# Attention with two mixtures of experts on one core: one wide GpSimd product for the strided heads of batch 0

## The chip, the core and the metric

The kernel runs on one core of a Trainium2 chip. A core has five engines that work through queues of their own, in order: TensorE (PE in the profile; its weight loads are PEld), VectorE (DVE), ScalarE (ACT), GpSimd (POOL) and SyncE (SP), which here issues most of the transfers. The metric is the device time of one execution in microseconds; lower is better. The time given is the median of three runs.

## The reference, cut to what matters

Three stages follow each other. Only the first, the attention, is touched.

```python
def _attn_ref(q, k, v):                       # 4 batches, 8 heads, 576 positions, 64 wide
    scores = scale * np.matmul(q, k.transpose(0, 1, 3, 2))
    rel = pos[:, None] - pos[None, :]
    mask_local = (rel >= 0) & (rel < 32)
    mask_strided = (rel >= 0) & (pos[None, :] % 32 == pos[:, None] % 32)
    # heads 0-3 take mask_local, heads 4-7 mask_strided
    scores = np.where(masks[None], scores, -1e9)
    attn = softmax(scores)                    # with 1e-9 added to the sum
    return np.matmul(attn, v)

x = attn_out.transpose(0, 2, 1, 3).reshape(2304, 512)
x = _moe_ref(x, w_in, w_out, g_ln)            # x @ w_in, softmax gate, layer norm, @ w_out
return _moe2_ref(x, ...)                      # top-1 of 8 experts, relu MLP, scaled by the gate
```

A strided head attends only to positions with the same remainder by 32. In the kernel a strided head's 576 positions are read as 8 groups of 72; within a group, 4 residues of 18 positions each see each other.

## The kernel before

**Tiling.** The attention goes through heads in pairs, and each pair through four units (two sets of tiles, two heads). Batch 0 takes its strided pairs first (PAIRS[0] is 2, 3, 0, 1), so the first eight units of the program are strided units of batch 0, with four tiles of 72 x 72 each; the next eight are its local units with 96-row tiles. Then come batches 1 to 3, mixed with the first mixture of experts, and from some 375 us on the experts of the second.

**A strided unit of batch 0** is made by `compact` (line 327). TensorE computes for each tile only the four residue blocks of 18 x 18 (L335), one block in each group of 32 partitions. VectorE adds the mask (L342), takes the maximum (L344), subtracts it (L345); ScalarE takes the exponential (L347); VectorE sums (L349) and takes the reciprocal (L350). Then GpSimd spreads the blocks: four products (L353), one per residue, each over 32 partitions, write the 18 probabilities of a row into every fourth column of a buffer `spread` of 72 columns, which four memsets cleared once at the start (L693). The columns of the other residues stay zero.

**Its transposition** (`probs_T`, L424) is a matmul with the spread tile as weights and, as the moving operand, 72 of the 128 columns of the identity, read with a stride of 32 elements so that rows come out in the order of positions. ScalarE copies the result to SBUF (L432), and TensorE multiplies with v (L441). The result goes to xTH and xTL (L453, L454).

**What shares the queues.** While this runs, the two weight matrices w_in and w_out, which are stored as 64-bit floats, are loaded in pieces of 512 KB by SyncE (L217) into three buffers and split by ScalarE and VectorE (L223, L231, L232, L234, L242, L243); for three of the first w_out pieces the scaling L225 is GpSimd's. GpSimd also fills `zrow` (L183) and `tabi` (L186, L187), which take their turn in the same three buffers and which SyncE stores to memory (L198, L199) ahead of the w_out loads. The local units use GpSimd for their normalisation (L413).

**Order.** The program is written as a sequence of slots, but the order in which an engine's queue holds the instructions is set when the program is built, by a planner that simulates the instructions' times. What one instruction takes in that simulation can move others.

Of the kernel before, what the change touches and what calls it, by code (L numbers as in the profile page):

```python
# [9 lines left out]
F32 = mybir.dt.float32  # L10
# [4 lines left out]
ALU = mybir.AluOpType  # L15
AX = mybir.AxisListType
# [12 lines left out]
def tile_attention_moe_moe2(  # L29
# [15 lines left out]
    nc = tc.nc  # L45
# [3 lines left out]
    P = 128  # L49
# [5 lines left out]
    SP_ = S // SG  # L55
    EPS = 3
    PITCH = P + EPS + 1
    QUAD = 32
    RES = STRIDE // SG
    NR = SP_ // RES  # L60
# [47 lines left out]
    ident = cst.tile([P, P], F32, name="ident")  # L108
# [23 lines left out]
    def flip_tile(out_, in_, eye):  # L132
        return nc.tensor.transpose(out_, in_, eye)  # L133
# [8 lines left out]
    def build_masks():  # L142
        nc.gpsimd.memset(rebias, 2.0 ** -112)
        nc.gpsimd.memset(zeros, 0.0)
        for t in range(2):
            m = maskL[:QT, t]
            nc.gpsimd.memset(m, 0.0)
            nc.gpsimd.affine_select(
                out=m, in_=m, pattern=[[-1, P]], compare_op=ALU.is_ge,
                fill=NEG, base=STRIDE, channel_multiplier=1)  # L150
            nc.gpsimd.affine_select(
                out=m, in_=m, pattern=[[1, P]], compare_op=ALU.is_gt,
                fill=NEG, base=0, channel_multiplier=-1)
            if t == 0:
                nc.gpsimd.memset(m[:, 0:STRIDE], NEG)
        rank = mp.tile([P, 1], I32, name="rank", tag="e")
        rankf = mp.tile([P, 1], F32, name="rankf", tag="e")
        nc.gpsimd.iota(rank, pattern=[[0, 1]], base=0, channel_multiplier=1)
        nc.gpsimd.iota(maskC, pattern=[[1, NR]], base=0, channel_multiplier=0,
                       allow_small_or_imprecise_dtypes=True)  # L160
        nc.vector.tensor_scalar(rank, rank, QUAD - 1, None, ALU.bitwise_and)
        nc.vector.tensor_copy(rankf, rank)
        nc.vector.tensor_scalar(maskC, maskC, rankf, NEG, ALU.is_gt, ALU.mult)
        apart = mp.tile([SP_, SP_], I32, name="apart", tag="so")
        nc.gpsimd.iota(apart, pattern=[[-1, SP_]], base=P, channel_multiplier=1)
        nc.vector.tensor_scalar(apart, apart, STRIDE // SG - 1, None, ALU.bitwise_and)
        nc.vector.tensor_scalar(maskS, apart, 0, NEG, ALU.is_gt, ALU.mult)
        nc.gpsimd.affine_select(
            out=maskS, in_=maskS, pattern=[[-1, SP_]], compare_op=ALU.is_ge,
            fill=NEG, base=0, channel_multiplier=1)  # L170
# [157 lines left out]
    def compact(tiles, j, qT, kT):  # L328
        nt = len(tiles)
        sp_ = ps.tile([P, 4, P], F32, name="S", tag="h")  # L330
        for i, t in enumerate(tiles):
            q0 = (j * SG + t) // 2 * SP_
            for r in range(RES):
                q1, k1 = q0 + r, STRIDE + q0 + r
                nc.tensor.matmul(  # L335
                    sp_[r * QUAD:(r + 1) * QUAD, i, :NR], qT[:, q1:q1 + RES * (QUAD - 1) + 1:RES],
                    kT[:, t % 2, k1:k1 + RES * (NR - 1) + 1:RES], start=True, stop=True)
        exw, px = exs[turn[0] % len(exs)], spread[turn[0] % len(spread)]
        turn[0] += 1
        ex = exw[:, :nt, EPS + 1:EPS + 1 + NR]  # L340
        mx = st.tile([P, 4], F32, name="mx")
        nc.vector.tensor_tensor(  # L342
            ex, sp_[:, :nt, :NR], maskC.unsqueeze(1).to_broadcast([P, nt, NR]), ALU.add)
        nc.vector.reduce_max(mx[:, :nt], ex, axis=AX.X)  # L344
        nc.vector.tensor_tensor(  # L345
            ex, ex, mx[:, :nt].unsqueeze(2).to_broadcast([P, nt, NR]), ALU.subtract)
        nc.scalar.activation(ex, ex, AF.Exp, scale=SCALE)  # L347
        rd = st.tile([P, 4], F32, name="rd")
        nc.vector.reduce_sum(rd[:, :nt], exw[:, :nt, EPS:EPS + 1 + NR], axis=AX.X)  # L349
        nc.vector.reciprocal(rd[:, :nt], rd[:, :nt])  # L350
        for r in range(RES):
            rows = slice(r * QUAD, (r + 1) * QUAD)
            nc.gpsimd.tensor_tensor(  # L353
                px[rows, :nt, r:SP_:RES], ex[rows],
                rd[rows, :nt].unsqueeze(2).to_broadcast([QUAD, nt, NR]), ALU.mult)
        return px, P, SP_, None

    def scores(b, hp, tiles, j, qT, kT):
# [58 lines left out]
    def probs_T(tiles, ex, nq, nk, den):  # L417
        nt = len(tiles)
        pt = ps.tile([P, 4, P], F32, name="pP", tag="T")
        if den is None:  # L420
            cols = ident.rearrange("p (r a) -> p a r", a=QUAD)[:, 0:NR, :]
            nq = nk
            for i in range(nt):
                nc.tensor.matmul(  # L424
                    pt[:nk, i, :nq].rearrange("p (a r) -> p a r", r=RES), ex[:, i, :nk], cols,
                    start=True, stop=True)
        else:
            for i in range(nt):
                flip_tile(pt[:nk, i, :nq], ex[:nq, i, :nk], ident[:nq, :nq])
        pT = at.tile([P, 4 * SP_], F32, name="pT", bufs=3)  # L430
        pT = pT[:, 0:nt * nq].rearrange("p (t q) -> p t q", q=nq)
        nc.scalar.copy(pT[:nk, :nt, :nq], pt[:nk, :nt, :nq])  # L432
        return pT
# [22 lines left out]
    def attention_slots():  # L456
# [25 lines left out]
        def stage_a(n):  # L482
            if n < len(units):
                b, hp, tiles, j = units[n]
                if b == 0 and hp >= H // 4:
                    live[n] = compact(tiles, j, *tr[n // 4])
                else:
                    live[n] = scores(b, hp, tiles, j, *tr[n // 4])
                    normalise(b, hp, len(tiles), *live[n])
# [8 lines left out]
        def stage_p(n):  # L498
            z = n - LAG
            if 0 <= z < len(units):  # L500
                b, hp, tiles, j = units[z]
                ex, nq, nk, den = live.pop(z)
                pts[z] = (probs_T(tiles, ex, nq, nk, den), nk if den is None else nq, nk)
# [179 lines left out]
    at = atstack.enter_context(tc.tile_pool(name="at", bufs=2))  # L683
# [4 lines left out]
    spread = []  # L688
    for i in range(2):
        pair = mp.tile([P, 2, 4, SP_], F32, name=f"spread{i}", tag="nL")  # L690
        spread.extend([pair[:, 0], pair[:, 1]])
    for x in spread:
        nc.gpsimd.memset(x, 0.0)  # L693
    kzs = [at.tile([P, 2, STRIDE + S], F32, name=f"kz{i}", bufs=1) for i in range(2)]
    for kz in kzs:
        nc.vector.memset(kz[:, :, 0:STRIDE], 0.0)
# [11 lines left out]
    def take(upto):  # L708
        nonlocal taken
        while taken < upto:  # L710
            next(slots, None)
            taken += 1

    build_masks()
    wout = list(range(KF))
    for i, at_ in enumerate(W_IN_AT):
# [629 lines left out]
```

## Time and profile before

| | us |
|---|---|
| median of three runs | 653.43 |
| the three runs | 651.59, 653.43, 659.1 |
| profiled execution, its own time | 650.67 |
| its span, first to last instruction | 649.0 |
| TensorE busy in the span | 606.4 (93%) |
| VectorE busy | 363.7 (56%) |
| ScalarE busy | 315.1 (49%) |
| GpSimd busy | 180.4 (28%) |

All rows quoted here come from that one profiled execution. Times in them count from the start of the span. A name such as L353 is a line of the kernel before. In a row, `out<-in` names what an instruction writes and reads, and a bracket at the end tells how long its engine idled before it and what ended the wait. A busy share is an average over stages that differ much, so the stretches are read one by one.

### The profile page before, as it was taken

The numbers are of one execution on the slowest core, as the hardware profiler recorded it, in microseconds if no ns is written. First come the engines' busy times: TensorE is split into PE (matmuls) and PEld (weight loads), VectorE is DVE, ScalarE is ACT, GpSimd is POOL, SyncE is SP. The second block draws the span as 40 slices with busy tenths as digits, with TensorE's granted clock in tenths as the row PEclk, the third lists the DMA queues.
The fourth block names the chain that finished last, engine by engine and source line by source line (L and its number), as shares of the span: only waits on it lengthen the run. The fifth ranks groups of instructions, "written<-read, shape, count | busy, mean of one in ns | idle before, by whom it ended". The sixth has DMA issues, their size and how long they took to land. (4 is left out here: it accounts for less than half of the span.)

```text
span 649.0 us, 13048 instructions
## 1 busy us (share of the span) xinstructions
PE 606.4 (93%) x4760; PEld 545.8 (84%) x4760; DVE 363.7 (56%) x1155; ACT 315.1 (49%) x685; POOL 180.4 (28%) x256
## 2 busy tenths in 40 slices
PE   5777999999999999999999999999999999999992
PEld 3666888999998988988888999989888888899892
DVE  5987698577767767667479753216354553121120
ACT  4679676567655667567356431224335352221220
POOL 4765364012432342112004312410121213012101
PEclk9997889999999999999999999999999999999997
DMA  8875221033211212110035300344546553012010
GB/s 219 207 216 146 77 84 38 19 88 100 74 54 37 70 43 77 54 36 3 27 106 178 99 34 19 103 163 129 183 135 207 144 202 101 20 49 66 19 47 24
DMA packets 54770, 59.97 MB, mean 92 GB/s; under 512 B 39312, under 2 KB 39312, under 8 KB 54674
## 3 DMA queue, kind: packets, MB, share of 16 engines
q1 hardware_dynamic: 47810, 42.52, 23.0%
q0 software_dynamic: 4272, 11.57, 5.7%
q10 hardware_dynamic: 2592, 4.72, 2.0%
q8 instruction: 46, 0.75, 0.5%
q14 instruction: 50, 0.41, 0.2%
HBM read 49.05 MB, written 10.26 MB: 91 GB/s over the span
## 5 line engine op out<-in xcount | busy, mean ns | idle before, releaser
L930 PE MATMUL py<-w2H,winL 128*128 128x512 f32 x288 | 92.1, 395 | 0.0
L970 PE MATMUL pf<-xTH,w1H 128*128 128x256 f32 x288 | 82.2, 286 | 1.4 <-ACT yo L1068 1.4
L970 PE MATMUL pf<-xTL,w1H 128*128 128x256 f32 x288 | 81.7, 284 | 0.7 <-DVE xTL L909 0.7
L970 PE MATMUL pf<-xTH,w1L 128*128 128x256 f32 x288 | 81.4, 283 | 0.0
L977 DVE SCALAR_TENSOR_TENSOR winL<-pf,winL 128x512 fp32r<-128x512 f32 x36 | 24.9, 691 | 94.4 <-ACT winL L976 94.3
L976 ACT ACTIVATE winL<-pf 128x512 fp32r<-128x512 f32 x36 | 21.5, 598 | 85.9 <-PE pf L970 85.2
L930 PEld LDWEIGHTS py<-w2H,winL 128*128 128x128 f32 x288 | 53.4, 188 | 10.6
L413 POOL TENSOR_TENSOR ex<-ex,rd 96x384 f32<-96x384 f32 (+1 forms) x48 | 40.5, 844 | 73.9 <-DVE rd L407 45.7
L536 PE MATMUL ph<-winH,xTH 128*128 128x512 f32 x144 | 58.6, 407 | 1.3 <-ACT xTH L453 0.8
L970 PEld LDWEIGHTS pf<-xTH,w1H 128*128 128x128 f32 x288 | 56.1, 195 | 3.1 <-issue 1.9
L536 PE MATMUL ph<-winL,xTH 128*128 128x512 f32 x144 | 57.6, 400 | 0.0
L970 PEld LDWEIGHTS pf<-xTL,w1H 128*128 128x128 f32 x288 | 56.2, 195 | 1.3 <-DVE xTL L909 1.1
L536 PE MATMUL ph<-winH,xTL 128*128 128x512 f32 x144 | 56.5, 399 | 0.0
L970 PEld LDWEIGHTS pf<-xTH,w1L 128*128 128x128 f32 x288 | 56.2, 195 | 0.0
L372 PE MATMUL S<-kz,qT 128*96 128x128 f32 (+1 forms) x384 | 48.2, 266 | 6.2 <-ACT kz L326 4.7
L936 POOL DMA_INDIRECT out_dram<-yo,idx x14 | 14.1, 1005 | 143.0 <-ACT yo L935 125.6
L372 PEld LDWEIGHTS S<-kz,qT 128*96 128x96 f32 (+1 forms) x384 | 41.6, 165 | 8.6 <-ACT kz L326 5.3
L391 POOL TENSOR_TENSOR ex<-ex,mx 96x384 f32<-96x384 f32 (+1 forms) x32 | 25.3, 791 | 81.7 <-DVE mx L387 40.2
L595 PE MATMUL pa<-woH,nH 128*128 128x264 f32 x144 | 42.1, 292 | 1.2 <-ACT nH L584 1.2
L595 PE MATMUL pa<-woH,nL 128*128 128x264 f32 x144 | 42.5, 295 | 0.0
L595 PE MATMUL pb<-woH,nL 128*128 128x256 f32 x144 | 41.1, 285 | 0.0
L595 PE MATMUL pb<-woL,nH 128*128 128x256 f32 x144 | 41.0, 284 | 0.0
(262 smaller groups left out, 1610.0 us busy)
## 6 DMA issues: line engine op xcount, KB each, us to landing
raw<-in_moe_w_dram SPq DMA_DIRECT2D x36, 512.0 KB, 3.6
y_d<-yt ACTq DMA_DIRECT2D x18, 256.0 KB, 2.2
raw<-in_moe_w_in_dram SPq DMA_DIRECT2D x8, 512.0 KB, 6.8
raw<-in_moe_w_out_dram SPq DMA_DIRECT2D x8, 512.0 KB
vn<-in_v_dram SPq DMA_DIRECT2D x16, 160.0 KB, 3.3
qn<-in_q_dram SPq DMA_DIRECT2D x8, 288.0 KB
kn<-in_k_dram SPq DMA_DIRECT2D x8, 288.0 KB
vn<-in_v_dram SPq DMA_DIRECT2D x8, 288.0 KB
```

The lines of the kernel that those rows point to most:

```text
L372: nc.tensor.matmul(sp_[:nq, i, :nk], qT[:, q0:q0 + nq], kT[:, half, k0:k0 + nk], start=True, stop=True)
L391: eng.tensor_tensor(ex[:nq, :nt, :nk], ex[:nq, :nt, :nk], mx[:nq, :nt].unsqueeze(2).to_broadcast([nq, nt, nk]), ALU.subtract)
L413: nc.gpsimd.tensor_tensor(ex[:nq, :nt, :nk], ex[:nq, :nt, :nk], rd[:nq, :nt].unsqueeze(2).to_broadcast([nq, nt, nk]), ALU.mult)
L536: nc.tensor.matmul(ph, a[:, c, ts_], w[:, c, cs], start=n == 0, stop=n == 3 * KD - 1)
L595: nc.tensor.matmul(p, a[:, f], w[:, f, cols], start=n == 0, stop=n == 3 * KF - 1)
L930: nc.tensor.matmul(p, a[:, f, s], x, start=n == 0, stop=n == 3 * KF - 1)
L936: nc.gpsimd.indirect_dma_start(out=out[:, :], out_offset=indirect(idx[:, col, 2:3].bitcast(U32)), in_=o, in_offset=None, bounds_check=NT - ...
L970: mm = nc.tensor.matmul(p[:, u], a[:, c, fs], x[:, c], start=n == 0, stop=n == 3 * KD - 1)
L976: last[0] = (nc.scalar.activation(hH[:, f2s], p, AF.Relu), nc.vector.scalar_tensor_tensor(hL[:, f2s], p, 0.0, hH[:, f2s].bitcast(F32), ALU ...
L977: nc.vector.scalar_tensor_tensor(hL[:, f2s], p, 0.0, hH[:, f2s].bitcast(F32), ALU.max, ALU.subtract))
```

## The change

GpSimd's four products per strided unit of batch 0 become one product over all 128 partitions. It computes all four columns of each group of four, and its second factor `rdm` holds the reciprocal for the row's own residue and zero for the other three; `rdm` is made by a new VectorE product of the reciprocal with a constant `own` (128 x 4, one where the partition belongs to the residue). As every column is written, the four memsets of `spread` go. The 72 columns of the identity that L424 reads with a stride are copied once into a dense constant `sel`, which the transposing matmuls then read.

```diff
@@ build_masks
+        nc.gpsimd.tensor_copy(
+            sel.rearrange("p (a r) -> p a r", r=RES),
+            ident.rearrange("p (r a) -> p a r", a=QUAD)[:, 0:NR, :])
+        nc.vector.reduce_sum(own, ident.rearrange("p (r a) -> p r a", a=QUAD), axis=AX.X)
@@ compact
-        for r in range(RES):
-            rows = slice(r * QUAD, (r + 1) * QUAD)
-            nc.gpsimd.tensor_tensor(
-                px[rows, :nt, r:SP_:RES], ex[rows],
-                rd[rows, :nt].unsqueeze(2).to_broadcast([QUAD, nt, NR]), ALU.mult)
+        rdm = at.tile([P, 4, RES], F32, name="rdm")
+        nc.vector.tensor_tensor(
+            rdm[:, :nt], rd[:, :nt].unsqueeze(2).to_broadcast([P, nt, RES]),
+            own.unsqueeze(1).to_broadcast([P, nt, RES]), ALU.mult)
+        nc.gpsimd.tensor_tensor(
+            px[:, :nt].rearrange("p t (a r) -> p t a r", r=RES),
+            ex.unsqueeze(3).to_broadcast([P, nt, NR, RES]),
+            rdm[:, :nt].unsqueeze(2).to_broadcast([P, nt, NR, RES]), ALU.mult)
@@ probs_T
-            cols = ident.rearrange("p (r a) -> p a r", a=QUAD)[:, 0:NR, :]
             nq = nk
             for i in range(nt):
-                nc.tensor.matmul(
-                    pt[:nk, i, :nq].rearrange("p (a r) -> p a r", r=RES), ex[:, i, :nk], cols,
-                    start=True, stop=True)
+                nc.tensor.matmul(pt[:nk, i, :nq], ex[:, i, :nk], sel, start=True, stop=True)
@@ where the buffers are made
-    for x in spread:
-        nc.gpsimd.memset(x, 0.0)
+    own = at.tile([P, RES], F32, name="own", bufs=1)
+    sel = at.tile([P, SP_], F32, name="sel72", bufs=1)
```

The pool `at` gives a tile two buffers unless it says otherwise, so `rdm` has two.

## Rows read from the trace of the kernel before

**Rows 1.** Stage windows: length, each engine's busy time (instructions), clock, DMA share, GB/s
```profile
20.00:40.00 20.00, 16.30 (x219) 14.34 (x219) 19.89 (x58) 15.35 (x34) 17.32 (x32) 1.00 0.72 205
...
80.00:375.00 295.00, 287.97 (x2389) 260.21 (x2389) 214.43 (x779) 182.26 (x428) 87.56 (x111) 0.99 0.23 65
375.00:649.00 274.00, 258.50 (x1709) 234.45 (x1708) 89.94 (x165) 77.68 (x133) 48.89 (x49) 0.98 0.31 97
```

**Rows 2.** Tile spread: ns min/median/max, first and last start; who waited for it
```profile
L353 POOL TENSOR_TENSOR spread<-ex,rd x32: 313/626/823, 14.1 to 39.6; 32x72 f32<-32x72 f32 x32
L693 POOL MEMSET spread<- x4: 328/338/342, 1.0 to 2.2; 128x288 f32 x4
...
  PEld pP L424: 3.1, 2
```

**Rows 3.** GpSimd's time line: start, length, operation, idle before and its end
```profile
23.41 12.46 POOL L353 TENSOR_TENSOR spread<-ex,rd 32x72 f32<-32x72 f32 x20
...
36.87 0.61 POOL L187 MEMSET tabi<- 128x176 int32 x1
...
43.91 1.04 POOL L225 TENSOR_TENSOR mag<-raw,rebias 128x512 f32<-128x512 f32 x1 [3.98 <-DMA raw<-in_moe_w_out_dram]
```

**Rows 4.** TensorE's time line
```profile
30.05 1.23 PE L424 MATMUL pP<-ident,spread 128*72 128x72 f32 x8 [1.81 <-ACT pT L432]
...
35.77 1.23 PE L424 MATMUL pP<-ident,spread 128*72 128x72 f32 x8 [0.92 <-ACT pT L432]
36.82 1.49 PE L372 MATMUL S<-kz,qT 128*96 128x128 f32 x6
...
38.59 0.87 PE L372 MATMUL S<-kz,qT 128*96 128x128 f32 x6
...
40.04 1.21 PE L424 MATMUL pP<-ident,spread 128*72 128x72 f32 x8
...
63.10 0.71 PE L133 MATMUL pP<-ident,ex 96*128 96x96 f32 x3 [1.36 <-ACT pT L432]
```

**Rows 5.** ScalarE's time line
```profile
34.67 0.68 ACT L223 ACTIVATE mag<-raw 128x512 f32<-128x512 f32 x1 [0.16 <-DMA raw<-in_moe_w_in_dram]
35.25 0.38 ACT L432 COPY pT<-pP 72x288 f32<-72x288 f32 x1
```

**Rows 6.** GpSimd's groups by shape, whole span: busy us, mean ns, idle before
```profile
L413 POOL TENSOR_TENSOR ex<-ex,rd 72x288 f32<-72x288 f32 x16 | 10.6, 664 | 38.3 <-DVE rd L407 21.8 <-PE ph L536 6.2 <-DVE nb L397 4.1
```

**Rows 7.** VectorE's lines in 0 to 42 us: ns min/median/max, first and last start
```profile
L231 DVE TENSOR_SCALAR wf<-mag x8: 408/481/697, 12.5 to 36.5; 128x512 int32<-128x512 int32 x8
...
L345 DVE TENSOR_TENSOR ex<-ex,mx x8: 217/330/459, 8.9 to 33.6; 128x72 f32<-128x72 f32 x8
...
L344 DVE TENSOR_REDUCE mx<-ex x8: 189/212/227, 8.6 to 32.4; 128x4 f32<-128x72 f32 x8
...
L234 DVE SCALAR_TENSOR_TENSOR wf<-raw,wf x8: 677/734/836, 14.0 to 38.6; 128x512 int32<-128x512 int32 x8
...
L243 DVE TENSOR_TENSOR winL<-wf,winH x8: 678/734/798, 16.3 to 40.1; 128x512 fp32r<-128x512 f32 x8
```

**Rows 8.** SyncE's time line: issues of transfers
```profile
39.06 2.87 SPq L217 DMA_DIRECT2D raw<-in_moe_w_out_dram  x3
```

**Rows 9.** VectorE's time line
```profile
8.33 0.23 DVE L342 TENSOR_TENSOR ex<-S,maskC 128x72 f32<-128x72 f32 x1 [2.85 <-PE S L335]
...
27.12 0.16 DVE L350 RECIPROCAL rd<-rd 128x4 f32<-128x4 f32 x1
27.21 0.19 DVE L344 TENSOR_REDUCE mx<-ex 128x4 f32<-128x72 f32 x1
...
38.56 0.79 DVE L234 SCALAR_TENSOR_TENSOR wf<-raw,wf 128x512 int32<-128x512 int32 x1
```

**Rows 10.** TensorE alone in two windows: length, busy (instructions), granted clock, DMA share, GB/s
```profile
62.60:69.40 6.80, 6.30 (x37) 0.50 0.32 82
83.10:86.50 3.40, 3.40 (x12) 0.50 0.26 57
```

## The prediction

> **What bounds the kernel.** I read the stage windows first, for where each engine is full; then the waits around the tile that the change rewrites; then the time lines of 14 to 46 us engine by engine, since each engine works its queue in order.
>
> The windows [rows 1] show two kernels in one. From 80 us on TensorE is busy 287.97 of 295 us and 258.50 of 274: no GpSimd work there is touched, so the change can only move the moment at which TensorE becomes full. Before that, in 20 to 40 us, VectorE is busy 19.89 of 20.00, TensorE 16.30, GpSimd 17.32. The reader is to see that VectorE, not GpSimd, has no room: its queue holds, besides the strided heads' softmax, the four operations per piece that split w_in.
>
> GpSimd comes second. The 32 small products of L353 take a median of 626 ns, 313 at best [rows 2]; twenty stand back to back for 12.46 us, so a unit (four of them) costs 2.49, and the zrow and tabi memsets, which end at 37.48, stand behind the last of them [rows 3]. TensorE's weight loads waited for these products twice, 3.1 us in all [rows 2]. But at 35.77 us the matmuls themselves wait for ScalarE [rows 4]: its copy of the transposed probabilities runs 35.25 to 35.63, behind an activation that a w_in transfer released [rows 5]. The other wait, at 30.05, is of that kind too [rows 4].
>
> **The change part by part.** *GpSimd.* Four products of 32 partitions x 72 become one of 128 x 288. The nearest row has 288 elements per partition and a broadcast factor: 664 ns [rows 6]. It doesn't have an input that repeats each element four times, or VectorE beside it. Bounds for a unit: 0.66, and today's 2.49. I take 1.0: 0.66 plus half of a split operation of some 0.68 (the best L234 and L243, [rows 7]) that it finds on its port. That removes 8 x (2.49 - 1.0) = 11.9 us of GpSimd work, nearly all of it beside VectorE's full queue.
>
> What of it comes through? First, the two TensorE waits: at most 3.1 us; as ScalarE's copies end at almost the same moments, I take 0.5 (ends 0 and 3.1). Second, SyncE. The first three w_out loads, issued from 39.06 to 41.93 [rows 8], stand behind the stores of zrow and tabi, and GpSimd idles 3.98 us until the first lands at 43.9 [rows 3]. With a shorter GpSimd queue the two memsets can start earlier, but tabi's buffer is released by VectorE and the first w_out load needs the buffer of the last w_in piece, whose last reader ends at 38.56 + 0.79 = 39.35 [rows 9]. So 0 to 0.8 us; I take 0.4.
>
> *VectorE, added.* Eight products of 16 elements for rdm. The nearest small operation is L350, 0.16 us long; the next one starts 0.09 us behind it (27.12 to 27.21, [rows 9]). The upper end is the best whole L345, 217 ns [rows 7]. I take 0.13 each, six of the eight in the full stretch: +0.8 us (ends 0.5 and 1.3). Their place is between reciprocal and product, so what is queued behind them is the splitting of w_in, for which the next loads on SyncE wait.
>
> *The port.* Several of VectorE's operations are stretched beside GpSimd's: L345 217 at best and 330 at the median, L231 408 and 481, L234 677 and 734, L243 678 and 734, while the reduction L344 stays within 189 to 227 [rows 7]. Eight times the differences is 8 x (113 + 73 + 57 + 56) = 2.4 us over the eight units. Afterwards a unit still moves 4 x 72 = 288 elements, in one stretch instead of four. If the stall follows the elements, it stays 2.4 us: I take that, 0 of change. Ends: no stall left, -2.4; every wide product stops VectorE for its whole 0.66, 8 x 0.66 - 2.4 = +2.9.
>
> [...]
>
> *TensorE.* The eight matmuls of a unit that transpose by picking columns take 1.23 us at 35.77 and 1.21 at 40.04, though their neighbours L372 go from 1.49 to 0.87 for six in between [rows 4]. Something other than the clock paces them; the strided read of the identity is the candidate. With dense columns at L372's faster pace, 0.87 / (6 x 128) x 8 x 72 = 0.65, a unit saves 0.56; at the slower pace 1.49 / 768 x 576 = 1.12, it saves 0.1. Two units run at the faster pace: 2 x 0.56 + 6 x 0.1 = 1.7 us. Only the one at 40.04 has TensorE working without a gap on both sides: I take 0.5 (ends 0 and 1.7).
>
> *At nothing.* Four memsets of spread (338 ns each, done by 2.6 us, [rows 2]) go; the copy into sel and the sum into own come. VectorE waits 2.85 us for the first scores at 8.33 [rows 9], which covers them; uncovered, each costs about its own length, some 0.3 us.
>
> *A wait that is added.* rdm has two buffers, so VectorE's rdm of one unit waits for the wide product two units before, and w_in's splitting behind it. Units come every 20/6 = 3.3 us; at 1.0 per product it is never late.
>
> **Sum.** +0.8 + 0 - 0.5 - 0.4 - 0.5 = -0.6 us. The profiled execution took 650.67 us (span 649.0): 650.1. The median of the three timed runs is 2.76 above it (653.43; 651.59 to 659.1), so 652.8 us.
>
> One uncertainty has no row: the order on each engine is made by a planner that simulates times when the program is built, so a unit that looks shorter to it can move everything near it. That widens each case by about the two TensorE waits, 3 us.
>
> **The rivals.** [...]
>
> *VectorE pays (slower).* Each wide product stops VectorE for its whole 0.66 us and rdm costs its upper end: +2.9 + 8 x 0.22 = +4.7, with no gain elsewhere: 658.1 us. For it: VectorE is full and gets eight operations more. Against it: the stretches of 0.1 us. [...] It passes 1% (6.5 us) from a hold of (6.5 - 1.8 + 2.4) / 8 = 0.9 us per product on.
>
> *The product doesn't get cheaper.* The pattern with four repeats may run as slowly as four products, 2.49 us. Then only rdm and the matmuls count: +0.8 - 0.5, 653.7 us.
>
> **Numbers.** The forecast has 0.60, with its own range 650 to 655.5; ahead of the clock 0.13; VectorE pays 0.17; not cheaper 0.10. The range of all, 647 to 658.5, leaves out nearly all of the 0.13 and the upper third of the 0.17. Faster or slower by over 1%, about what a measurement of this kernel can tell, means below 646.9 or above 660: 0.13 and 0.07; within it 0.80.
>
> **What would show it.** Right: eight products near 1.0 us, GpSimd's busy time in 14 to 46 down by 10 us or more while VectorE stays full in 20 to 40; eight matmuls of a unit at about 0.65 us where the clock is full; the first w_out landing within 1 us of 43.9. Wrong: products over 2 us (not cheaper); L234 or L345 longer by 0.3 or more beside a product (VectorE pays); full clock in 62 to 69 us (ahead of the clock); or the end of that low stretch, at 69.4 us, moved by 3 us or more with none of these, which would be the planner's order.

## The result, and the profile after

The changed kernel takes 661.0 us (median of 17 runs, 657.53 to 664.64) against 653.5 for the kernel before (17 runs, 649.31 to 659.1): ratio 1.0113, with a 95% interval of 1.0091 to 1.0136. It is slower by 7.5 us, clear of the noise and outside the range of 647.0 to 658.5. The profiled execution of after took 660.0 us, with a span of 658.3.

The lines that answer to [rows 1], the stage windows of after (columns: window and length, then busy time of PE, PEld, DVE, ACT and POOL with their instructions, granted clock, DMA share, GB/s):

```profile
20.00:40.00 20.00, 13.55 (x193) 11.92 (x193) 18.04 (x56) 13.84 (x30) 10.75 (x13) 1.00 0.82 211
80.00:375.00 295.00, 285.63 (x2330) 257.13 (x2331) 208.44 (x753) 175.72 (x413) 81.86 (x107) 0.98 0.21 61
375.00:658.00 283.00, 266.26 (x1761) 241.88 (x1759) 95.72 (x189) 82.13 (x143) 51.90 (x53) 0.98 0.31 99
```

GpSimd is down from 17.32 to 10.75 us in 20 to 40, as the change wanted. But TensorE is busy 2.3 us less in 80 to 375 us, a stretch in which no operation was changed. The lines of the new product and of rdm (ns min/median/max, first and last start), which answer to [rows 2], and those of VectorE's operations that answer to [rows 7] (L235 is L231 of before, L238 is L234, L247 is L243, L349 is L345):

```profile
L359 POOL TENSOR_TENSOR spread<-ex,rdm x8: 848/1047/1570, 15.0 to 38.9; 128x288 f32<-128x288 f32 x8
L356 DVE TENSOR_TENSOR rdm<-rd,own x8: 154/160/408, 14.7 to 38.6; 128x16 f32<-128x16 f32 x8
L235 DVE TENSOR_SCALAR wf<-mag x15: 386/420/1129, 12.2 to 92.6; 128x512 int32<-128x512 int32 x15
L238 DVE SCALAR_TENSOR_TENSOR wf<-raw,wf x16: 658/678/1014, 13.7 to 112.3; 128x512 int32<-128x512 int32 x16
L247 DVE TENSOR_TENSOR winL<-wf,winH x8: 674/687/887, 16.0 to 43.1; 128x512 fp32r<-128x512 f32 x8
L349 DVE TENSOR_TENSOR ex<-ex,mx x8: 191/220/233, 8.5 to 32.8; 128x72 f32<-128x72 f32 x8
```

The product has its 1.05 us, and the stretches of VectorE's operations are gone at the median (the rows of L235 and L238 go on to 112 us; up to 42 us their medians are 420 and 677 as well). They are not gone at the longest ones; the part on the prediction comes back to that. The strided units did not become slower: what follows them starts 0.81 us earlier. Where the time went is seen by putting the first matmul of each token tile of the first mixture of experts (moe_a) of both traces side by side:

| first matmul of moe_a | before, us | after, us | difference |
|---|---|---|---|
| t=1 | 82.11 | 81.29 | -0.81 |
| t=2 | 96.28 | 100.33 | +4.05 |
| t=3 | 107.40 | 112.40 | +5.00 |
| t=4 | 131.89 | 138.18 | +6.29 |
| t=17 | 355.47 | 361.48 | +6.01 |

After is ahead when the last strided unit is long done, loses 7 us between 81 and 138 us, and keeps that to the end. About 0.7 us of the 7 (an estimate) lies at none of the places that follow: a stretch of half clock at the start of t=1 reaches 4.9 us past that start in after (79.3 to 86.2 us) and 3.4 us in before (83.1 to 86.5). (Another 3.3 us between 442 and 484 us, among the experts, is not the change: before's profiled execution took 37.65 us for that piece, and the eleven other kernels of this study took 38.6 to 41.7, whatever their order. The six longest of the twelve, after among them, each have 3.4 us of half clock there.)

Two waits of TensorE in that stretch are new. Its time line in after (start, length, operation; in brackets the idle time before it and what ended it; pP and pn are transpositions, pg a gate group, po the product with v, ph the matmuls of moe_a):

```profile
92.19 0.45 PE L133 MATMUL pP<-ident,ex 96*128 96x96 f32 x3
...
95.06 0.72 PE L445 MATMUL po<-pT,vn 128*64 128x96 f32 x12 [1.30 <-ACT pT L436]
...
105.00 1.84 PE L275 MATMUL pg<-wg,wt 128*128 128x8 f32 x16
106.70 0.45 PE L133 MATMUL pP<-ident,ex 96*128 96x96 f32 x3
106.98 0.60 PE L133 MATMUL pn<-ident,so 128*128 128x128 f32 x4
107.34 0.48 PE L540 MATMUL ph<-winH,xTL 128*128 128x512 f32 x1
...
108.89 0.72 PE L445 MATMUL po<-pT,vn 128*64 128x96 f32 x12
112.40 0.50 PE L540 MATMUL ph<-winH,xTH 128*128 128x512 f32 x1 [2.79 <-DVE so L555]
```

At 105.00 the queue holds two gate groups (pg), a transposition and half of another one ahead of the last four matmuls of t=2, which start at 107.34. In before the last of these matmuls goes ahead of both gate groups, and t=3 hardly waits:

```profile
103.09 0.48 PE L536 MATMUL ph<-winH,xTL 128*128 128x512 f32 x1
103.41 0.95 PE L271 MATMUL pg<-wg,wt 128*128 128x8 f32 x8
...
107.40 0.50 PE L536 MATMUL ph<-winH,xTH 128*128 128x512 f32 x1 [0.35 <-DVE so L551]
```

What depends on those four is the chain that t=3 waits for. VectorE's and ScalarE's rows of it in after:

```profile
108.85 0.68 DVE L544 TENSOR_REDUCE hmx<-ph 128x1 f32<-128x512 f32 x1
109.91 0.20 DVE L549 TENSOR_SCALAR hnb<-hmx 128x1 f32<-128x1 f32 x1
111.68 0.65 DVE L555 SCALAR_TENSOR_TENSOR so<-e,ph 128x512 f32<-128x512 f32 x1
```
```profile
110.15 0.69 ACT L552 ACTIVATE e<-ph,hnb 128x512 f32<-128x512 f32 x1
110.83 0.68 ACT L552 ACTIVATE e<-ph,hnb 128x512 f32<-128x512 f32 x1
```

The wait at 95.06 is of the same kind. The transposition at 92.19 was done by 92.7, but the copy of its result (L436) stood in ScalarE's queue behind the scaling of a w_out piece, for which ScalarE itself waited 2.17 us until VectorE had split the piece:

```profile
93.66 0.91 ACT L258 ACTIVATE woH<-wf,gln 128x256 fp32r<-128x256 f32 x2 [2.17 <-DVE wf L238]
94.47 0.25 ACT L277 ACTIVATE woH<-pg,gln 128x8 fp32r<-128x8 f32 x1
94.62 0.38 ACT L436 COPY pT<-pP 128x288 f32<-128x288 f32 x1
```

Some 1.1 to 1.3 us behind the end of each wait the granted clock falls to 0.50, while before runs at a granted clock of 1.00 from 86.5 us to its last 10 us. Windows of after over these two stretches, columns as above:

```profile
96.40:99.80 3.40, 3.08 (x17) 2.86 (x16) 3.40 (x16) 3.40 (x10) 2.22 (x2) 0.50 0.21 64
113.50:116.90 3.40, 3.40 (x10) 2.52 (x9) 1.95 (x10) 1.96 (x4) 0.55 (x1) 0.50 0.00 0
```

TensorE works through nearly all of both, and slower: four transpositions of 128 x 128 take 1.11 us at 97.91 in the first and 0.60 behind it at 99.97. So each stretch costs about half its busy time (an estimate), 1.5 to 1.7 us. None of these instructions was changed. What differs is the order in which the queues hold them.

### The profile page after: what moved, and what is told of

Same layout as the page of the kernel before. It is cut to its first block, busy times and chain, and to the rows that moved or that the text cites. A ratio compares the mean times of both kernels' runs of the same rounds, so it can differ in the third digit from the quotient of the medians.

```text
span 658.3 us, 13020 instructions
## 1 busy us (share of the span) xinstructions
PE 609.7 (93%) x4760; PEld 548.1 (83%) x4760; DVE 365.6 (56%) x1164; ACT 314.2 (48%) x685; POOL 169.2 (26%) x229
## 5 line engine op out<-in xcount | busy, mean ns | idle before, releaser
L420 POOL TENSOR_TENSOR ex<-ex,rd 96x384 f32<-96x384 f32 (+1 forms) x48 | 38.1, 795 | 77.7 <-DVE rd L414 51.1
L379 PE MATMUL S<-kz,qT 128*96 128x128 f32 (+1 forms) x384 | 49.1, 268 | 4.1 <-ACT kz L330 3.1
L379 PEld LDWEIGHTS S<-kz,qT 128*96 128x96 f32 (+1 forms) x384 | 42.6, 167 | 6.9 <-ACT kz L330 3.9
L599 PE MATMUL pa<-woL,nH 128*128 128x264 f32 x144 | 41.2, 286 | 0.0
```

The source lines that it names most:

```text
L379: nc.tensor.matmul(sp_[:nq, i, :nk], qT[:, q0:q0 + nq], kT[:, half, k0:k0 + nk], start=True, stop=True)
L420: nc.gpsimd.tensor_tensor(ex[:nq, :nt, :nk], ex[:nq, :nt, :nk], rd[:nq, :nt].unsqueeze(2).to_broadcast([nq, nt, nk]), ALU.mult)
L599: nc.tensor.matmul(p, a[:, f], w[:, f, cols], start=n == 0, stop=n == 3 * KF - 1)
```

## The experiments

Three theories. **A, the order:** the operations of after cost nothing, and the order that the planner makes of them costs some 7 us. **B, the operations:** the wide product, rdm or the constant of 72 columns cost the time themselves. **C, the clock:** the half-clock stretches come by chance. The ratio given for each run is the one of its own comparison and need not be the quotient of the two medians.

### Operations and order taken apart

The order of a queue can be forced: for each engine a list holds the order of the instructions ahead of the first branch (some 370 us of the span), and an issue-order edge goes from each to the next. The edges add no wait between engines.

```diff
@@ ahead of main_step(1)
+    traced = list(nc.cur_bb.bb.instructions)
+    for order in json.loads(zlib.decompress(base64.b64decode(ORDER))):   # one list per engine
+        for a, b in zip(order, order[1:]):
+            tc.add_manual_dep(
+                traced[b], traced[a].name,
+                mybir.DependencyInfo(mybir.DependencyClass.NoSync, mybir.DependencyReason.DATA),
+                reason="issue order")
     main_step(1)
```

*p_after_bo: after's operations in before's order.*

> The operations of after, with every engine's instructions up to the first branch queued in the order that the kernel before has (the wide product stands where one of the four narrow ones stood; own, sel and the eight rdm stand where the planner puts them). Theory A, the queue order: the loss of 7.5 us goes away, and the time is that of before less the 0.8 us that the strided units had gained by 81 us: about 652.7 us, ratio 0.997 to 1.003. Theory B, the operations themselves (the wide product's reads and writes, the eight extra VectorE products): the loss stays, 660 to 661 us, ratio 1.009 to 1.014. Theory C, the clock's own variation, whatever the order: the low stretches between 79 and 117 us (about 4 of the 7 us) stay, ratio about 1.006.

*p_before_ao: before's operations in after's order.*

> The operations of before (four narrow products and 72 strided identity columns), with every engine's instructions up to the first branch queued in the order that after has. Theory A, the queue order: slower by about as much as after, 659 to 662 us, ratio 1.009 to 1.014, with the wait ahead of the fourth moe_a tile near 112 us (2.79 us on a VectorE result in after) there too. Theory B, the operations: as before, ratio 0.998 to 1.002. Theory C: anywhere between.

Two more take the change in halves and leave the planner free. *e_sel* has the constant alone:

```diff
-            cols = ident.rearrange("p (r a) -> p a r", a=QUAD)[:, 0:NR, :]
...
-                nc.tensor.matmul(
-                    pt[:nk, i, :nq].rearrange("p (a r) -> p a r", r=RES), ex[:, i, :nk], cols,
-                    start=True, stop=True)
+                nc.tensor.matmul(pt[:nk, i, :nq], ex[:, i, :nk], sel, start=True, stop=True)
```

> Before with the 72 identity columns in a constant alone: narrow products stay, and the queue order is that of before throughout. Theory A: the 32 matmuls gain at most what the dense columns save, 32 x 0.1 to 0.6 us off the chain, so 0 to 1 us faster, ratio 0.998 to 1.000. Theory B: no loss either, unless the dense columns cost, which their 0.65 us at full clock does not suggest; ratio 0.998 to 1.002.

*e_wide* has the GpSimd product, own and rdm alone, that is the diff of after without the lines above.

> Before with the wide product, own and rdm alone (strided identity columns stay, the four memsets of the spread tiles are gone): the queue order is that of after on every engine. Theory A: the loss is there, ratio 1.008 to 1.014. Theory B: the loss is there as well if the wide product makes it, so this run tells only whether the constant of 72 columns has a part in it: 1.000 if the constant makes the loss, 1.011 if not.

| kernel | operations | order | median, us | ratio to before | 95% interval |
|---|---|---|---|---|---|
| before | before | before | 653.36 | | |
| p_after_bo | after | before | 653.42 | 0.9991 | 0.9967 to 1.0016 |
| e_sel | constant only | before | 653.63 | 0.9988 | 0.9963 to 1.0014 |
| p_before_ao | before | after | 659.27 | 1.0071 | 1.0052 to 1.0090 |
| after (first comparison) | after | after | 661.0 | 1.0113 | 1.0091 to 1.0136 |
| e_wide | product only | after | 663.04 | 1.0135 | 1.0098 to 1.0172 |

Theory B falls twice: after's operations in before's order take before's time, and before's operations in after's order are slower. C falls as the cause, since chance does not follow the order through six kernels. It has a part in single executions: the profiled one of p_after_bo, at 657.88 us the slowest of its twelve, has 3.4 us of half clock from 98.1 us on, in before's order. By the medians the order is worth 5.9 us with before's operations and 7.6 with after's; the operations are worth nothing that can be told in before's order. In after's order they may add something: p_before_ao's ratio of 1.0071 is below the 1.009 to 1.014 that was expected, and its interval ends below those of after and e_wide. Why is open. The two waits go with the order too. TensorE's rows in p_before_ao, where the operations are those of before (L582 is the po matmul and L677 the moe_a matmul there):

```profile
97.20 1.23 PE L582 MATMUL po<-pT,vn 128*64 128x96 f32 x12 [4.32 <-ACT pT L573]
...
114.58 0.50 PE L677 MATMUL ph<-winH,xTH 128*128 128x512 f32 x1 [2.80 <-DVE so L692]
```

The halves show which part moves the order. With the constant alone the planner made before's order on every engine; with the product alone, after's. Why the planner does so is open.

### The two places, one at a time

Here after keeps its own order, forced as above, but for a block of instructions that stand as in before. Theory A is split: **A1**, the two waits and the low clock at them are the loss; **A2**, the order loses the time elsewhere, ahead of them.

*h_112: the block from t=2's first matmul to t=4's.*

> After with its own queue order everywhere but between the first matmul of moe_a t=2 and the first of t=4 (100.3 to 138.2 us in after), where the instructions stand as in before: the last four matmuls of t=2 go ahead of the gate groups again. Theory A1, the waits are the loss: the 2.79 us that TensorE waits at 112.4 us for the VectorE result so goes away, and with it perhaps the half-clock stretch behind it (3.4 us at 0.50, worth 1.7 us): 661.0 - 2.8 = 658.2, down to 656.5; ratio to before 1.004 to 1.008. Theory A2, the loss was made ahead of here (in the order up to 100 us): 660 to 661.5 us, ratio 1.010.

*h_95: the block from t=1's first matmul to t=2's.*

> After with its own queue order everywhere but between the first matmul of moe_a t=1 and the first of t=2 (81.3 to 100.3 us in after), where the instructions stand as in before. Theory A1, the waits: the wait of the po matmuls for the pT copy near 95 us (1.30 us in after, 4.32 and 2.18 us in the two others with this order) goes away: 661.0 - 1.3 to 4.3 = 656.7 to 659.7 us; ratio 1.005 to 1.010. Theory A2, the price sits in the queues ahead of 81 us: no change, 661 us.

*h_both: both blocks, with after's order through the strided units.*

> After with before's order between the first matmul of moe_a t=1 and the first of t=4 (81.3 to 138.2 us in after) and its own order everywhere else, the strided units among it. Theory A1, these two waits and the low clock behind them are all of the loss: 653 to 655 us, ratio 0.999 to 1.003. Theory A2, the order ahead of 81 us carries the loss, for instance by the clock that it leaves: 658 to 661 us, ratio 1.006 to 1.011.

*e_after_mem* leaves the order to the planner and keeps four memsets, which makes it choose a third one:

```diff
+    for x in spread:
+        nc.gpsimd.memset(x, 0.0)
```

> After with the four memsets of the spread tiles kept: the same operations but for four memsets in the first 3 us on GpSimd, which write what the wide product overwrites. The planner makes a third order of it (some 200 places on TensorE's queue differ from either kernel's). Theory A, the queue order: a time of its own, anywhere from 651 to 664 us, not bound to after's 661. Theory B, the operations: that of after, 660 to 662 us, since four memsets of 0.3 us at the start delay nothing.

Then two small edits that a person might try. *m_edge2* lets two gate groups follow moe_a t=2:

```diff
@@ moe_a, behind the ph matmuls (mm is the last of them, gates holds each gate group's first matmul)
+        if t == 2:
+            for x in gates[-2:]:
+                queue_after(x, mm)
```

> After with one issue-order edge added by hand and the planner free around it: the two gate groups that stand ahead of the last four matmuls of moe_a t=2 must come behind them. The planner moves only the later of the two (on TensorE: 20 ph, one gate group, pP, half of pn, 4 ph, the other gate group) and then re-plans what follows. Theory A1, the waits: the VectorE result so comes about one gate group (0.95 us) and half a pn earlier, so the 2.79 us wait shrinks by about 1 us and the one near 95 us stays: 659 to 660.5 us, ratio 1.009; if the re-planning behind it hides the wait, 656 to 658 us. Theory B, the operations: 661 us.

*m_g66* changes the table that says at which call a gate is made:

```diff
-    GATE_AT = [1, 2, 2, 3, 3, 4, 4, 6]
+    GATE_AT = [1, 2, 2, 3, 3, 6, 6, 6]
```

> After with the hand-made table of gate calls changed, GATE_AT 3, 4, 4 to 3, 6, 6 for the sixth and seventh: the two gate groups then stand behind moe_a t=2 and in the middle of other work (TensorE: 20 ph, half of pn, po, 1 ph, pt, 3 ph, pt, gate, pt, gate). Theory A1: the last matmul of t=2 still stands behind pn and po, so a wait like that of 112 us stays, with the one near 95 us: 658 to 662 us, ratio 1.007 to 1.013. Theory B, the operations: 661 us. A time under 655 would show that moving the gates in the table is enough.

The table has all kernels, with TensorE's longest waits in the two places and the stretches of half clock that begin between 90 and 140 us, each from the kernel's one profiled execution. That need not be a typical one: those of h_95, m_edge2 and m_g66 are the fastest of their runs, those of p_after_bo, p_before_ao and e_after_mem the slowest.

| kernel | wait near 95, us | wait near 112, us | half clock begins at (length), us | median, us | ratio to before |
|---|---|---|---|---|---|
| before | under 0.5 | 0.35 | none | 653.4 | |
| e_sel | under 0.5 | 0.35 | none | 653.63 | 0.9988 |
| p_after_bo | 1.16 | 0.35 | 98.1 (3.4) | 653.42 | 0.9991 |
| h_both | under 0.3 | 0.35 | none | 653.91 | 1.0011 (0.9987 to 1.0035) |
| h_112 | 2.85 | 0.30 | 95.8 (6.8) | 655.93 | 1.0037 (1.0015 to 1.0059) |
| m_edge2 | 1.21, 0.83 | 2.14 | 111.6 (3.4) | 658.36 | 1.0076 (1.0049 to 1.0103) |
| h_95 | 0.85 | 2.80 | none | 658.56 | 1.0106 (1.0078 to 1.0134) |
| p_before_ao | 4.32 | 2.80 | 94.7 (6.8), 115.2 (3.4) | 659.27 | 1.0071 |
| m_g66 | 4.32 | 0.88, 0.52 | 93.3 (6.8) | 659.86 | 1.0108 (1.0058 to 1.0157) |
| after | 1.30 | 2.79 | 96.4 (3.4), 113.5 (3.4) | 661.0 | 1.0113 |
| e_wide | 2.18 | 2.80 | 99.1 (3.4), 116.1 (3.4) | 663.04 | 1.0135 |
| e_after_mem | 1.64 | 1.98 | 101.2 (6.8), 118.2 (3.4) | 663.24 | 1.0146 (1.0114 to 1.0179) |

The two places together are the loss. Mending both gives 661.0 - 653.91 = 7.1 us, and what is left, 653.91 against 653.26 us with an interval on both sides of one, is the whole price of after's order ahead of 81 us. Mending the one near 112 gives 661.0 - 655.93 = 5.1 us, more than the 2.8 to 4.5 that were expected of it. The one near 95 is less sure: alone it gives 2.4 us by the medians, within what was expected, but h_95's own ratio of 1.0106 is hardly below after's 1.0113; on top of the other, from h_112 to h_both, it gives 2.0.

How much of the 5.1 us is the clock can be estimated from the mean granted clock of every run: 0.977 over after's 17 runs and 0.980 over h_112's 12, which over 660 us is some 2 us, next to a wait that is shorter by 2.5. The rows of a single profile do not add up to a median: h_112's has a wait of 2.85 us and 6.8 us of half clock left, some 6 us by themselves, and its median is 2.7 us above before's. And a block is more than its wait; what else its order changes was not told apart. In h_112 the last four matmuls of t=2 stand ahead of the gates again, and t=3 hardly waits:

```profile
108.06 0.39 PE L681 MATMUL ph<-winH,xTL 128*128 128x512 f32 x1
108.30 0.95 PE L416 MATMUL pg<-wg,wt 128*128 128x8 f32 x8
...
112.24 0.50 PE L681 MATMUL ph<-winH,xTH 128*128 128x512 f32 x1 [0.30 <-DVE so L696]
```

While h_both runs at full clock and nearly without a gap through the stretch in which after lost 7 us:

```profile
88.00:138.00 50.00, 49.23 (x404) 44.65 (x403) 36.74 (x132) 29.03 (x73) 17.66 (x21) 1.00 0.15 43
```

e_after_mem shows how little it takes: four memsets in the first 3 us, and the planner's third order is, with e_wide, the slowest of all. (It does not part theory A from B, whose 660 to 662 us overlap with its interval.) The small edits regained 2.6 us (m_edge2, between the two outcomes that were expected) and 1.1 us (m_g66, as expected, and not clear of noise), because the planner arranged the rest anew around them: m_edge2 has the wait near 112 in another place, for a VectorE operation of a w_out piece, and m_g66 has 4.32 us near 95. No kernel here beats the one before; p_after_bo and h_both, the change with a good order, equal it.

## Why the prediction was wrong, step by step

**The sum fits the operations, as far as that can be told.** It forecast -0.6 us. p_after_bo has these operations and before's order, and its ratio of 0.9991 is -0.6 us, with -2.2 to +1.0 as the interval; its median is 0.06 us above before's. So an effect much over 2 us is unlikely, and the agreement to a tenth is luck. Some terms under the sum were off and made up for each other:

- *GpSimd.* 1.0 us per product was taken, 1.05 is the median. The eight together take 9.2 us in after's time line, against 19.2 for the four groups of small products in before's: 10.0 saved of the 11.9 forecast. Nothing that can be told of that comes through, which fits the first part, where GpSimd comes second.
- *rdm.* 0.16 us at the median against 0.13 taken. The eight last 1.5 us in all in after, as some are stretched; the upper end was 1.3, for six.
- *The port.* No change was taken. That the two engines share a port was the author's assumption, and half of a split operation lost there (0.34 of the 1.0 us) an estimate: the rows show only how long the operations took. The medians fell by 110 ns (L349), 61 (L235), 56 (L238) and 47 (L247) against [rows 7], together 8 x 0.274 = 2.2 us, near the lower end of -2.4. But the medians mislead, for the stretches became fewer and longer. The time that VectorE's operations beside a product took over the shortest of their kind in three traces (13 to 42 us) adds up to 3.2 us in before, 2.3 in after and 2.8 in p_after_bo: most of it stayed, so "no change" was nearer than either end. Either engine can be the one that is stretched. In p_after_bo one operation of VectorE takes 0.90 us, against 0.43 at its line's median, beside a product of 1.24; and one product is 2.05 us long, while VectorE's operations at its side are close to their shortest times. GpSimd's rows and VectorE's:

```profile
26.80 1.24 POOL L500 TENSOR_TENSOR spread<-ex,rdm 128x288 f32<-128x288 f32 x1 [1.26 <-DVE rd L494]
...
33.42 2.05 POOL L500 TENSOR_TENSOR spread<-ex,rdm 128x288 f32<-128x288 f32 x1 [2.33 <-DVE rdm L497]
```
```profile
27.43 0.90 DVE L376 TENSOR_SCALAR wf<-mag 128x512 int32<-128x512 int32 x1
...
33.52 0.67 DVE L379 SCALAR_TENSOR_TENSOR wf<-raw,wf 128x512 int32<-128x512 int32 x1
...
34.27 0.67 DVE L377 SCALAR_TENSOR_TENSOR wf<-raw,wf 128x512 int32<-128x512 int32 x1
```

  Which of the two engines is held, these rows do not settle (the product that starts at 33.42 is stretched, the operation that starts behind it at 33.52 is not), and no run changed the order of issue alone.
- *TensorE.* Dense columns gave nothing at the slower pace and some 0.5 us per unit at the faster one (0.65 was taken for the unit, 0.74 came):

```profile
37.89 1.21 PE L430 MATMUL pP<-sel,spread 128*72 128x72 f32 x8 [1.25 <-ACT pT L436]
38.89 1.53 PE L379 MATMUL S<-kz,qT 128*96 128x128 f32 x6
...
42.64 0.74 PE L430 MATMUL pP<-sel,spread 128*72 128x72 f32 x8
```

- *SyncE.* The first w_out piece landed 0.5 us earlier (0.4 was taken), as GpSimd's row says that answers to the 43.91 of [rows 3]:

```profile
43.40 1.26 POOL L229 TENSOR_TENSOR mag<-raw,rebias 128x512 f32<-128x512 f32 x1 [2.90 <-DMA raw<-in_moe_w_out_dram]
```

**The step that failed is the planner's order.** The prediction named it, gave it "about the two TensorE waits, 3 us" as a widening of each case, and gave it neither a case nor a chance of its own. It measured 7.6 us with after's operations and 5.9 with before's, to one side both times. Behind that is a sentence of the first part: that from 80 us on no GpSimd work is touched, "so the change can only move the moment at which TensorE becomes full". The operations there were indeed untouched. Their order was not, since the planner makes one order for all, and a full TensorE (97.6% busy in 80 to 375 us) is just where a worse order has nothing to hide behind. The size was mis-read too. The two waits that were taken for it stood in the strided units, where VectorE was the full engine (what a TensorE wait costs there no run shows); behind 80 us the place with the wait of 2.8 us cost 4.7 us (h_95 against h_both) to 5.1 (after against h_112), more than the wait itself.

**The rivals.** "VectorE pays" gave 658.1 us, near the measured time, by a mechanism that did not happen to that extent: single operations of VectorE beside a product were longer by 0.2 to 0.5 us than the shortest of their kind, in all no longer than before, and the same operations took 653.42 us in another order. "Ahead of the clock", the faster case with 0.13, had its sign, a granted clock of 1.00 in 62.6 to 69.4 us against the 0.50 of [rows 10], and no gain: after has a stretch at 0.51 from 79.3 to 86.2 us instead. That a TensorE kept fed keeps its full clock, no run shows: in before it is busy 3.40 of 3.40 us at 0.50 [rows 10]. "Not cheaper" is out by the 1.05 us.

**The signs.** Products near 1.0 and the first w_out piece within 1 us came as written. GpSimd's busy time in 14 to 46 us fell by 8.6 us instead of 10. VectorE stayed full in 20 to 40 us in before's order (19.80 us in p_after_bo) but not in after's (18.04). Of the sign of "VectorE pays", 0.3 us more beside a product, the nearest for these lines is one L379 (L234 of before) of 1.03 us in p_after_bo, against 0.68 at the median; whether a product ran beside it was not shown, and the price did not come. The sign for the order was the weak one: it looked at the end of one low stretch, which depends on the clock as well. The start of each moe_a tile would have been the sign to name.

## What to carry to other kernels

Where a planner orders the queues by simulated times, an edit has two effects, its own and that of the new order, and they can be told apart by forcing the old order onto the new operations; that should come before any story on the operations. Ahead of a change, ask at which places the old order has a full engine with almost no wait (here 0.35 us at t=3), and price the loss of that fit as a case of its own, at the length of the dependent chain (there a wait of 2.8 us, and 4.7 to 5.1 with what came behind it) and not at that of the waits now seen. Work saved on an engine that comes second may be worth nothing: here 10 us of GpSimd's time gave nothing that could be told.

## What the runs showed of the hardware

**The place with TensorE's wait of 2.8 us cost 4.7 to 5.1 us.** In the table, 14 waits are longer than 1.1 us, and next to 12 of them the granted clock is at 0.50 for 3.4 or 6.8 us; no such stretch begins between 90 and 140 us without a wait like that. The exceptions are h_95's 2.80 us and m_edge2's 1.21. The wait alone does not decide it: among the experts all twelve kernels have a wait for the same matmul, of 1.45 to 2.11 us between 460 and 474 us, and 3.4 us of half clock begin next to it in six of them, in either order, and in the other six not. What makes the difference is open. It fits with mending the place near 112 being worth 5.1 us where the wait is 2.8.

**The same wait comes out to 10 ns.** In the four kernels with after's order behind t=2 it is 2.79, 2.80, 2.80 and 2.80 us, with different operations far ahead of it: so it looks like the length of a dependent chain, not an accident of the run.

**A granted clock of 1.00 can stand for no record.** In after, three transpositions of 96 x 96 take 0.69 us at 40.21 and 0.41 at 43.21, and the profile shows 1.00 for the clock in windows around both. But the clock records of after's trace begin at 41.8 us, and those of before's at 38.7, so the first window's 1.00, and that of 20 to 40 us in [rows 1], measure nothing or next to nothing. TensorE's faster pace began between the two transpositions, near 42 us; what held it before is not shown.

```profile
40.21 0.69 PE L133 MATMUL ptq<-ident,qn 96*128 96x96 f32 x3
...
43.21 0.41 PE L133 MATMUL ptq<-ident,qn 96*128 96x96 f32 x3
```
```profile
39.00:41.50 2.50, 2.50 (x14) 2.50 (x14) 2.47 (x9) 1.51 (x4) 1.50 (x3) 1.00 0.75 170
42.50:45.00 2.50, 2.50 (x33) 2.31 (x28) 2.50 (x9) 2.50 (x7) 1.26 (x1) 1.00 0.78 261
```
